# The second layer of six of nine expert blocks in three float32r passes, with the weights split on chip

## The chip, the cores and the metric

One core of one Trainium2 chip runs the whole program in one launch. The metric is the device time of an execution in microseconds (us), the median of several; lower is better. TensorE is called PE below (PEld its weight loads), VectorE DVE, ScalarE ACT, GpSimd POOL, SyncE SP.

## What is computed

Three parts run one after the other on 1536 tokens (two batches of 768): attention with a window and a few sink keys, a mixture of eight experts with one expert per token, and a two-layer network with an exponential unit. In the reference's own names, cut:

```python
# attention, 2 x 8 heads, 768 x 64: keep = sink (pos < 4) or window (0 <= rel < 128)
a = softmax(where(keep, q @ k.T / 8, -1e9));  x = (a @ v) as [1536, 512]
# experts: only tokens with x @ w_skip > 0; one expert each
for e in range(8):                     # w1[e]: 512 x 1024, w2[e]: 1024 x 512
    h = maximum(x[mask] @ w1[e], 0.0)
    y[mask] = gate_w[mask, None] * (h @ w2[e])
x[do_compute] += y
# network: w_in 512 x 2048, w_out 2048 x 512
h = x @ w_in;  g = where(h > 0, h, exp(minimum(h, 0)) - 1);  out = g @ w_out
```

The inputs are float32, but `w_in` and `w_out` arrive as float64, 8 bytes an element.

## The kernel before

**Stages.** Attention goes over 12 tiles of 128 tokens and writes x to a table in DRAM (`xtab`). Then come nine blocks of 128 tokens: one for each of the eight experts, and a ninth (e = 8, `last`) for an expert with more than 128 tokens. Then the network runs in four groups of 512 tokens; each goes through 16 chunks of 128 hidden columns (`layers`: `l1`, the exponential unit `elu`, `l2`).

**One block** (`block`). Its 128 rows are gathered from `xtab` (`gather`, POOL), transposed on PE (`bx`, line 460) and copied to SBUF (`bxe`, line 345). The first layer (`b1`, line 902) is two halves of 16 float32 matmuls with 128 columns; `relu` (lines 910 and 912) takes each half out of PSUM, on ACT or DVE. The second layer (`b2`, line 918) is eight float32 matmuls of 128x512, in two halves of four; the transposes of the next block stand between the halves. `result` (line 933) scales and adds the rows on DVE, `scat` writes them back. The trace shows each float32 matmul as two records, so a half of `b2` is 8 records and a half of `b1` is 32. In block 8 the second layer goes over the two halves of the output columns one after the other (matmuls of 128x256), so that the next stage can begin on the first.

**Weights.** A block has eight tiles of 128x1024 float32 (512 KB): four of w1, four of w2. They live in half places: `places` are 16 buffers of 128x2048, and `halves` their 32 halves. Places 0 to 11 are there from the start; 12 to 15 hold attention's small tiles (`spare`) and are opened when attention ends (`aend`). Six more tiles (`exs`, in `exa` and `exb`) and the four `raw` tiles take some weights too.

**The network's weights.** Each chunk's `w_in` and `w_out` are loaded as float64 into a `raw` tile (`load_f`, lines 736 and 738) and turned into two float32r parts by seven steps (`cv`): ACT reads the high word (line 970), DVE does lines 972, 973, 974 and 976, then a cast to the high part (line 978, ACT or DVE) and the low part as a subtraction (line 290). The products of the network are three float32r matmuls each, `PASSES` = high·high, high·low, low·high (lines 1089 and 1127).

**Start of the network.** Group 0 reads its x from `xtab` (`load_x0`, line 1000, behind the scatter of block 7), transposes it (`x0t`, line 1040), and adds what block 8 changed by two more products (`x0b`, `x0a`, line 1044) of a one-hot matrix with the change in two parts (`dl`, lines 1013 and 1015). Then `split` cuts it into parts (`xe`, lines 1029 and 1031).

**What sets the order.** Every step is named in a plan with its engines, its length, what it follows, its buffers and a due time (`prio`). A list scheduler (`Plan.run`) picks engine, order and buffers from these numbers when the program is built; on the chip each engine goes through its own list in order, and semaphores do the waiting. So a changed length or due time moves other steps as well.

Of the kernel before, what the change touches and what calls it, by code (L numbers as in the profile page):

```python
# [8 lines left out]
F32 = mybir.dt.float32  # L9
# [8 lines left out]
P = 128  # L18
# [40 lines left out]
class Plan:  # L59
# [116 lines left out]
def fused_kernel(  # L176
# [112 lines left out]
    def sub(o, a, b, e):  # L289
# [13 lines left out]
        xg=ring(4, INF), xT=ring(2, INF), hT=ring(2, INF), a=ring(2, INF), r=ring(2), g=ring(3), XT=ring(6), row=ring(6, INF), o2=raws,  # L303
    )
    kinds["R"] = raws
    pl = Plan(kinds)
# [33 lines left out]
    def sl(kind_tiles, key):  # L340
        return kind_tiles[pl.slot[key][1]]
# [421 lines left out]
    opened = halves[2 * NPA:] + exs + [s for n in ("xg", "xT", "hT", "a") for s in kinds[n] if n != "a" or not s[1]]  # L763
# [83 lines left out]
    def first_block():  # L847

        gl = len(GROUPS) - 1
        nl = GROUPS[gl]  # L850
        t0 = NTILE - nl
        add("gid0", {"d": 0.2}, lambda e: nc.vector.tensor_copy(out=gid0, in_=tab[:, 0:1]), [("g", gl - 1, "tab")], 9.3)
        pl.by["g", gl, "mx"]["after"].append("gid0")
        er = lambda: places[NPA + 1][:, 0:DG]

        def early(e):
            nc.gpsimd.indirect_dma_start(
                out=er(), out_offset=None, in_=xtab[0:1 + t0 * P, :],
                in_offset=bass.IndirectOffsetOnAxis(ap=gid0[:, 0:1].bitcast(U32), axis=0),
            )  # L860
        add("early", {"p": 1.1}, early, ["gid0", "zst"] + [("st", x) for x in range(t0)] + [("g", x, "st") for x in range(gl)], 9.4, lat=3.2)

        def gathered(e):
            for i in range(KD):
                nc.tensor.matmul(bk(("bx", 0), 4)[:, i, :], er()[:, i * P:(i + 1) * P], ident, start=(i == 0), stop=False, is_transpose=True)
        add("bx00", {"e": 0.44}, gathered, ["early", ("av", NTILE - 1, 1)], 11.25, need=[("S", ("bx", 0), 1)])
        for i in range(nl):
            t = t0 + i

            def hot(e, i=i):  # L870
                nc.vector.scalar_tensor_tensor(out=hot0[i], in0=iota, scalar=g8["t"][:, i, 0:1], in1=goh[:, i, 0:1].to_broadcast([P, P]), op0=ALU.is_equal, op1=ALU.mult)
            add(("hot0", i), {"d": 0.26}, hot, [("g", gl, "t8")], 11.2)
# [4 lines left out]
            add(("bx", 0) if i == nl - 1 else ("bxo", i), {"e": 0.9}, own, [("bxo", i - 1) if i else "bx00", ("hot0", i), ("fx", t, 0), ("fx", t, 1)], 11.3, use=[("x", t)])  # L877

    def block(e):
        p0 = 20.0 + 10.0 * e  # L880
# [15 lines left out]
        for n in range(2):  # L896
            def layer1(eng, n=n):
                o = bk(("h", e, n), 4)
                for i in range(4):
                    f = 4 * n + i  # L900
                    for kk in range(KD):
                        nc.tensor.matmul(o[:, i, :], w_tile(("w", e, kk))[:, f * P:(f + 1) * P], sl(post["xT"], ("xT", e))[:, kk, :],  # L902
                                         start=(i == 0 and kk == 0), stop=(i == 3 and kk == KD - 1))
            add(("b1", e, n), {"e": 3.55}, layer1, [("bxe", e)] + [("w", e, kk) for kk in range(KD)], p0 + n, need=[("HB", ("h", e, n), 1)],
                use=[("xT", e)] + [("w", e, kk) for kk in range(KD)])

            def relu(eng, n=n):
                o, i = sl(post["hT"], ("hT", e))[:, 4 * n:4 * n + 4, :], bk(("h", e, n), 4)
# [4 lines left out]
            add(("relu", e, n), {"a": 0.6, "d": 0.69}, relu, [("b1", e, n)] + ([("relu", e, 0)] if n else []), p0 + n, need=[] if n else [("hT", ("hT", e), 2)], use=[("h", e, n)])  # L913

            def layer2(eng, fs, c):
                for f in fs:
                    w = w_tile(("w", e, KD + f // 2)).rearrange("p (c n) -> p c n", c=2)[:, f % 2, :]
                    nc.tensor.matmul(bk(("y", e))[:, c], sl(post["hT"], ("hT", e))[:, f, :], w[:, c], start=(f == 0), stop=(f == KF - 1))  # L918
            ws = [("w", e, KD + 2 * n + i) for i in range(2)]
            if not last:  # L920
                add(("b2", e, n), {"e": 3.45}, lambda eng, n=n: layer2(eng, range(4 * n, 4 * n + 4), slice(0, DM)), [("relu", e, n)] + ws + ([("b2", e, 0)] if n else []), p0 + 2 + n,
                    need=[] if n else [("Y", ("y", e), 1)], use=[("hT", e)] + ws)
            else:

# [34 lines left out]
    for c in range(NCH):  # L959
        gate_c = [("b2", c, 1)] if c < NB - 1 else [("b1", NB - 1, 1)]  # L960
        for w in range(2):
            p0 = 24.0 + 10 * c + w if c < 8 else 300 + (c - 8) * 1.0 - 3.0 + 0.5 * w
            f = ("f", c, w)
            add(("lf", c, w), {"s": 0.45}, lambda e, c=c, w=w: load_f(c, w), [chain[-2]], p0 - 12, need=[("R", f, 2)], size=524288)
# [22 lines left out]

    def piece(g, kk):

        i, j = divmod(pl.slot["XT", g, kk][1], 3)  # L990
        if i not in xt_tiles:
            t = post["bp"].tile([P, 3072], F32R, tag=("a", "xh")[i], name=f"xT{i}")
            xt_tiles[i] = t.rearrange("p (j a n) -> p j a n", j=3, a=2)
        return xt_tiles[i][:, j]
# [524 lines left out]
```

## Time and profile before

| | |
|---|---|
| three executions | 536.35, 538.21, 538.85 us; median 538.21 us |
| profiled execution | 538.53 us, of which the profile's span is 536.7 us |
| busy share of the span | PE 96%, PEld 77%, DVE 59%, ACT 33%, POOL 6% |
| mean granted clock of PE | 0.994 |

The span runs from the first to the last instruction. Attention fills it up to about 128 us, the nine blocks to about 262 us, the four groups of the network the rest. A row of the timeline gives start, length, engine, line, operation, operands and how many were merged; the length holds the drain of the last matmul, so the time of a piece is read from its start to the start of the next piece.

### The profile page before, as it was taken

The page shows a single profiled execution, that of the slowest core. Times are in us where ns is not written, and L with a number is a line of the kernel's source. Part 1 is how long each engine was busy: PE and PEld are TensorE (multiplying, and loading weights), DVE is VectorE, ACT ScalarE, POOL GpSimd, SP SyncE. Part 2 cuts the span into 40 slices and gives each one's busy share as a digit, 9 for nine tenths or more (in the row PEclk, how much of TensorE's full clock was granted, in tenths as well). Part 3 has the DMA queues.
Part 4 walks back from the last instruction along what each step waited for, and adds up shares of the span by engine and source line. Part 5 has one row for each costly group of instructions (what it writes and reads, how often), then busy time and mean ns, then how long its engine had stood idle before and what let it go on. Part 6 is the DMA issues. An engine that isn't in the chain of part 4 may idle for free. (4 is left out here: it accounts for less than half of the span.)

```text
span 536.7 us, 8226 instructions
## 1 busy us (share of the span) xinstructions
PE 512.6 (96%) x3087; PEld 411.5 (77%) x3087; DVE 317.5 (59%) x848; ACT 175.6 (33%) x421; POOL 32.2 (6%) x47
## 2 busy tenths in 40 slices
PE   6899999997999999999999999999999999999993
PEld 3678777877777777778788888888888888888882
DVE  6768686876212278886998944454444545445451
ACT  4777677751000123434486520220101112010110
POOL 2000000012110111000000000100000010000000
PEclk9999999998999999999999999999999999999998
DMA  9999999309999967856474000220000002000002
GB/s 171 255 250 309 311 281 336 95 25 342 396 393 395 349 200 237 295 177 197 159 233 157 1 1 0 77 80 1 0 1 0 1 1 79 1 1 0 1 0 85
DMA packets 73155, 79.11 MB, mean 147 GB/s; under 512 B 43089, under 2 KB 51537, under 8 KB 73106
## 3 DMA queue, kind: packets, MB, share of 16 engines
q1 hardware_dynamic: 69826, 73.29, 43.7%
q0 software_dynamic: 1520, 4.99, 2.6%
q8 instruction: 26, 0.43, 0.3%
q10 hardware_dynamic: 1760, 0.22, 0.3%
q14 instruction: 23, 0.19, 0.1%
HBM read 69.82 MB, written 8.66 MB: 146 GB/s over the span
## 5 line engine op out<-in xcount | busy, mean ns | idle before, releaser
L1127 PE MATMUL bank<-m,gt 128*128 128x512 f32 x576 | 139.1, 390 | 0.0
L1089 PE MATMUL bank<-xT,m 128*128 128x512 f32 x576 | 138.3, 389 | 0.0
L1089 PEld LDWEIGHTS bank<-xT,m 128*128 128x128 f32 x576 | 108.1, 188 | 22.5
L1127 PEld LDWEIGHTS bank<-m,gt 128*128 128x128 f32 x576 | 107.8, 188 | 22.2
L1107 ACT ACTIVATE re<-re 128x512 f32<-128x512 f32 x48 | 30.3, 632 | 174.6 <-DVE re L1105 174.4
L1105 DVE TENSOR_SCALAR re<-bank 128x512 f32<-128x512 f32 x38 | 26.3, 692 | 83.7 <-PE bank L1089 83.7
L902 PEld LDWEIGHTS bank<-blk,pl 128*128 128x128 f32 x480 | 55.3, 192 | 3.7 <-issue 2.6
L918 PE MATMUL bank<-pl,blk 128*128 128x512 f32 (+1 forms) x144 | 57.8, 545 | 0.0
L902 PE MATMUL bank<-blk,pl 128*128 128x128 f32 x480 | 56.1, 275 | 0.7 <-ACT blk L345 0.7
L545 ACT ACTIVATE pw<-sm,rm 128x272 f32<-128x272 f32 (+2 forms) x96 | 47.1, 495 | 7.7 <-DVE rm L537 7.7
L1110 DVE SCALAR_TENSOR_TENSOR re<-re,bank 128x512 f32<-128x512 f32 x48 | 32.9, 686 | 26.5 <-ACT re L1107 26.5
L918 PEld LDWEIGHTS bank<-pl,blk 128*128 128x128 f32 x144 | 26.2, 190 | 20.9 <-issue 20.1
L970 ACT ACTIVATE r<-raw 128x512 f32<-128x512 f32 x32 | 21.3, 680 | 61.8 <-DMA raw<-in_moe_w_in_dram 52.3
L537 DVE CUSTOM_DVE_ANT_0 sm<-bank,mk 128x272 f32<-128x272 f32 (+2 forms) x96 | 35.1, 406 | 6.5 <-PE bank L531 3.8
L290 DVE TENSOR_TENSOR gt<-re,gt 128x512 fp32r<-128x512 f32 x44 | 30.4, 692 | 1.3
L531 PE MATMUL bank<-kt,pl 64*128 64x272 f32 (+2 forms) x192 | 26.8, 394 | 1.3 <-DVE rm L537 1.3
L345 ACT COPY PT<-bank 128x512 f32<-128x512 f32 (+1 forms) x40 | 20.6, 550 | 13.4 <-PE bank L559 11.1
L572 PE MATMUL bank<-PT,pl 128*64 128x128 f32 x352 | 24.5, 279 | 0.1
L572 PEld LDWEIGHTS bank<-PT,pl 128*64 128x64 f32 x352 | 18.7, 136 | 5.6 <-issue 3.0
L460 PE MATMUL bank<-ident,pl 128*128 128x128 f32 x96 | 14.8, 279 | 7.8 <-DMA pl<-in_k_dram 5.6
L290 DVE TENSOR_TENSOR m<-r,m 128x512 fp32r<-128x512 f32 x32 | 21.5, 687 | 0.9 <-ACT m L978 0.6
L976 DVE SCALAR_TENSOR_TENSOR r<-raw,r 128x512 int32<-128x512 int32 x32 | 21.8, 687 | 0.3
(186 smaller groups left out, 513.7 us busy)
## 6 DMA issues: line engine op xcount, KB each, us to landing
pl<-in_moe_w_dram SPq DMA_DIRECT2D x62, 512.0 KB
raw<-in_moe_w_in_dram SPq DMA_DIRECT2D x16, 512.0 KB
raw<-in_moe_w_out_dram SPq DMA_DIRECT2D x16, 512.0 KB
pl<-in_k_dram SPq DMA_DIRECT2D x12, 256.0 KB
pl<-in_q_dram SPq DMA_DIRECT2D x12, 256.0 KB
pl<-in_v_dram SPq DMA_DIRECT2D x12, 256.0 KB
xtab<-pl SPq DMA_DIRECT2D x12, 256.0 KB
out_dram<-raw SPq DMA_DIRECT2D x5, 512.0 KB
```

Source lines behind the costliest of these rows:

```text
L290: CE[e].tensor_tensor(out=o, in0=a, in1=b, op=ALU.subtract)
L531: nc.tensor.matmul(o, qT[r, p, :], rhs, start=True, stop=True)
L537: nc.vector.tensor_tensor_reduce(out=sl(sm_t, ("sm", t, h))[:, 0:n], in0=bk(("s", t, h))[:, 0:n], in1=m, scale=-scale, scalar=3.0e38, op0= ...
L545: nc.scalar.activation(out=sl(pw_t, ("pw", t))[:, h, 0:n], in_=sl(sm_t, ("sm", t, h))[:, 0:n], func=ACTF.Exp, bias=rm[:, t, h:h + 1], scal ...
L572: nc.tensor.matmul(o[i * D:(i + 1) * D, p, :], vt[:, h * D:(h + 1) * D], pT[:, (0 if y else c - 2) + i, :], start=(p == 0 and (y == 1 or n ...
L902: nc.tensor.matmul(o[:, i, :], w_tile(("w", e, kk))[:, f * P:(f + 1) * P], sl(post["xT"], ("xT", e))[:, kk, :], start=(i == 0 and kk == 0) ...
L918: nc.tensor.matmul(bk(("y", e))[:, c], sl(post["hT"], ("hT", e))[:, f, :], w[:, c], start=(f == 0), stop=(f == KF - 1))
L1089: nc.tensor.matmul(bk(name), w[:, a, kk, :], x[:, b], start=(kk == 0 and i == 0), stop=(kk == KD - 1 and i == 2))
L1105: nc.vector.tensor_scalar(out=r, in0=pt, scalar1=-1.0, scalar2=0.0, op0=ALU.mult, op1=ALU.max)
L1107: nc.scalar.activation(out=r, in_=r, func=ACTF.Exp, scale=-1.0)
L1110: nc.vector.scalar_tensor_tensor(out=r, in0=r, scalar=-1.0, in1=pt, op0=ALU.add, op1=ALU.max)
L1127: nc.tensor.matmul(bk(("acc", g, i)), gt[:, a, i * P:(i + 1) * P], w[:, b, :], start=(c == 0 and j == 0), stop=(c == NCH - 1 and j == 2))
```

## The change

For six blocks, e in `RB` = 1, 2, 3, 4, 5 and 8, the second layer becomes three float32r passes. Each w2 tile is cut on the chip into a high part (`hi`, a cast, ACT or DVE) and a low part (`lo`, a subtraction on DVE), kept as one tile `hl` of 128x2x1024 float32r in places 12 to 15: four `hl` tiles, as many as one block has, opened when block 0's `bx` is done and no longer used for weights until block 8 ends. `relu` gives the high part of h on ACT, a new step `rell` on DVE the low part. Blocks 0, 6 and 7 stay in float32. A w2 tile is free again when its low part is made, no longer when the matmuls have read it. The due times of the conversions (`cv`) go from 24 + 10c for the first eight chunks to 297 + c for all, those of their loads to 12 + 10c; the tiles of the expert stage are laid out anew (`xa`, `xb`, `hs`). The core of the diff:

```diff
+    RB = (1, 2, 3, 4, 5, 8)
-    opened = halves[2 * NPA:] + exs + [s for n in ("xg", "xT", "hT", "a") ...]
+    opened = exs + [s for n in ("xg", "xT", "hT", "a") ...]
...
+    def hl(key):
+        i = pl.slot[key][1]
+        if i not in hl_tiles:
+            hl_tiles[i] = place_p.tile([P, 2048], F32R, tag=f"pl{i}", name=f"hl{i}").rearrange("p (a n) -> p a n", a=2)
+        return hl_tiles[i]
...
+            if fine:
+                def relu_low(eng, n=n):
+                    h = sl(post["hT"], ("hT", e, n))
+                    nc.vector.scalar_tensor_tensor(out=h[:, 1], in0=bk(("h", e, n), 4), scalar=0.0, in1=h[:, 0].bitcast(F32), op0=ALU.max, op1=ALU.subtract)
+                add(("rell", e, n), {"d": 0.7}, relu_low, [("relu", e, n)], p0 + n, use=[("h", e, n)])
+                for i in (2 * n, 2 * n + 1):
...
+                    add(("hi", e, i), {"a": 1.02, "d": 0.66}, lambda eng, key=key, wt=wt: CPY[eng](out=hl(key)[:, 0], in_=wt()), [("w", e, KD + i)], p0 - 5 + i, port=True, need=[("HL", key, 2 if last else 1)])
+                    add(("lo", e, i), {"d": 1.16}, lambda eng, key=key, wt=wt: sub(hl(key)[:, 1], wt(), hl(key)[:, 0].bitcast(F32), eng), [("hi", e, i)], p0 - 5 + i, port=True, use=[("w", e, KD + i)])
...
+                    if fine:
+                        w = hl(("hl", e, f // 2)).rearrange("p a (c n) -> p a c n", c=2)[:, :, f % 2, c]
+                        h = sl(post["hT"], ("hT", e, f // 4))
+                        for j, (a, b) in enumerate(PASSES):
+                            nc.tensor.matmul(y, h[:, a, f % 4, :], w[:, b], start=(f == 0 and j == 0), stop=(f == KF - 1 and j == 2))
...
-            p0 = 24.0 + 10 * c + w if c < 8 else 300 + (c - 8) * 1.0 - 3.0 + 0.5 * w
+            pf, p0 = (12.0 + 10 * c + w if c < 8 else 280 + c + 0.5 * w), 297 + c + 0.5 * w
```

**Where the order moves.** DVE between the first halves of the second layers of blocks 1 and 2, before: `blk` is the relu output or the transposed x, `r` the rows of a block.

```order
L912 TENSOR_SCALAR blk<-bank_90 128x512
L912 TENSOR_SCALAR blk<-bank_91 128x512
L345 COPY blk<-bank_96 128x512
L933 SCALAR_TENSOR_TENSOR r_1489<-bank_94,r_1489 128x512
L912 TENSOR_SCALAR blk<-bank_92 128x512
L912 TENSOR_SCALAR blk<-bank_89 128x512
```

The same place now; `hr` is h in parts, `hl` the split w2 tile, line 292 the subtraction, 938 the cast, 933 `rell`, 968 `result`.

```order
L933 SCALAR_TENSOR_TENSOR hr<-bank_90,hr 128x512
L933 SCALAR_TENSOR_TENSOR hr<-bank_91,hr 128x512
L938 CAST hl_1547<-pl_73 128x1024
L347 COPY blk<-bank_96 128x512
L292 TENSOR_TENSOR hl_1547<-pl_73,hl_1547 128x1024
L292 TENSOR_TENSOR hl_1550<-pl_73,hl_1550 128x1024
L968 SCALAR_TENSOR_TENSOR r_1491<-bank_94,r_1491 128x512
L292 TENSOR_TENSOR hl_1571<-pl_74,hl_1571 128x1024
L292 TENSOR_TENSOR hl_1578<-pl_74,hl_1578 128x1024
L933 SCALAR_TENSOR_TENSOR hr<-bank_92,hr 128x512
L933 SCALAR_TENSOR_TENSOR hr<-bank_89,hr 128x512
```

One cast and four subtractions of 128x1024 stand between the two blocks, around `result`; the other three casts are on ACT.

PE at the end of block 8, before: lines 1040 and 1044 are `x0t` and `x0b`/`x0a`, line 918 the second layer's second output half, 1089 the network.

```order
L1040 MATMUL bank_89<-ident,exb 128x128 x4
L1044 MATMUL bank_90<-oh,delta 128x512
L1044 MATMUL bank_91<-oh,delta 128x512
L918 MATMUL bank_93<-pl_64,blk 128x256 x4
L1044 MATMUL bank_90<-oh,delta 128x512
L1044 MATMUL bank_91<-oh,delta 128x512
L918 MATMUL bank_93<-pl_65,blk 128x256 x4
L1044 MATMUL bank_92<-oh,delta 128x512
L1044 MATMUL bank_89<-oh,delta 128x512
L1089 MATMUL bank_95<-xT_2269,m_1872 128x512 x6
L1044 MATMUL bank_92<-oh,delta 128x512
L1044 MATMUL bank_89<-oh,delta 128x512
```

The same place now; line 948 is the split second layer, 1076 `x0t`, 1080 `x0b` and `x0a`.

```order
L948 MATMUL bank_93<-hl_1571,hr 128x256 x6
L948 MATMUL bank_93<-hl_1578,hr 128x256 x6
L1076 MATMUL bank_90<-ident,exb 128x128 x4
L1076 MATMUL bank_91<-ident,exb 128x128 x4
L1076 MATMUL bank_92<-ident,exb 128x128 x4
L1076 MATMUL bank_89<-ident,exb 128x128 x4
L1080 MATMUL bank_90<-oh,delta 128x512
L1080 MATMUL bank_91<-oh,delta 128x512
L1080 MATMUL bank_92<-oh,delta 128x512
L1080 MATMUL bank_89<-oh,delta 128x512
L1080 MATMUL bank_90<-oh,delta 128x512
L1080 MATMUL bank_91<-oh,delta 128x512
```

The whole second layer of block 8 now stands ahead of the transposes of x; two more products of `x0a` and then the network follow.

## Rows read from the trace of the kernel before

**Rows 1.** Three stretches: length, busy us (records) by engine, clock, DMA share, GB/s.
```profile
128.61:244.33 115.72, 115.72 (x672) 84.72 (x673) 60.92 (x125) 23.20 (x38) 17.05 (x16) 1.00 0.86 308
244.33:264.39 20.06, 19.50 (x127) 17.39 (x126) 17.86 (x34) 8.35 (x15) 1.82 (x2) 1.00 0.58 197
264.39:350.00 85.61, 85.61 (x387) 71.04 (x386) 59.86 (x108) 36.22 (x61) 3.15 (x3) 1.00 0.24 77
```
**Rows 2.** Timeline of PE, second layer of block 1.
```profile
150.31 3.60 PE L918 MATMUL bank<-pl,blk 128*128 128x512 f32 x8
153.74 0.60 PE L460 MATMUL bank<-ident,r 128*128 128x128 f32 x4
154.18 3.60 PE L918 MATMUL bank<-pl,blk 128*128 128x512 f32 x8
```
**Rows 3.** Timeline of PE, the network in group 0.
```profile
290.28 2.88 PE L1089 MATMUL bank<-xT,m 128*128 128x512 f32 x12
293.00 2.88 PE L1127 MATMUL bank<-m,gt 128*128 128x512 f32 x12
```
**Rows 4.** Timeline of PE, block 8 and the start of group 0.
```profile
244.33 7.31 PE L902 MATMUL bank<-blk,pl 128*128 128x128 f32 x64
251.47 3.62 PE L918 MATMUL bank<-pl,blk 128*128 128x256 f32 x16
255.08 1.97 PE L1040 MATMUL bank<-ident,exb 128*128 128x128 f32 x16
256.80 0.71 PE L1044 MATMUL bank<-oh,delta 128*128 128x512 f32 x2
259.54 1.89 PE L918 MATMUL bank<-pl,blk 128*128 128x256 f32 x8
261.99 0.73 PE L1044 MATMUL bank<-oh,delta 128*128 128x512 f32 x2 [0.56 <-ACT delta L1013]
262.56 1.54 PE L1089 MATMUL bank<-xT,m 128*128 128x512 f32 x6
264.39 1.78 PE L1089 MATMUL bank<-xT,m 128*128 128x512 f32 x7
```
**Rows 5.** Groups by form: busy us, mean ns, idle us before, releaser.
```profile
L345 ACT COPY PT<-bank 128x512 f32<-128x512 f32 x33 | 18.1, 588 | 7.4 <-PE bank L559 6.4 <-ACT PT L345 0.5 <-ACT pw L545 0.3
L345 ACT COPY PT<-bank 128x256 f32<-128x256 f32 x7 | 2.5, 371 | 6.0 <-PE bank L559 4.7 <-issue 1.3
L1112 DVE CAST gt<-re 128x512 fp32r<-128x512 f32 x34 | 14.5, 427 | 1.2
L290 DVE TENSOR_TENSOR m<-r,m 128x512 fp32r<-128x512 f32 x32 | 21.5, 687 | 0.9 <-ACT m L978 0.6
L611 DVE TENSOR_TENSOR pl<-bank,den 128x256 f32<-128x256 f32 x24 | 10.1, 422 | 2.5 <-PE bank L603 2.0
L933 DVE SCALAR_TENSOR_TENSOR r<-bank,r 128x512 f32<-128x512 f32 x9 | 6.7, 749 | 11.1 <-PE bank L918 11.1
L910 ACT ACTIVATE blk<-bank 128x512 f32<-128x512 f32 x8 | 4.8, 597 | 20.7 <-PE bank L902 16.7 <-issue 3.9
L345 DVE COPY blk<-bank 128x512 f32<-128x512 f32 x4 | 2.8, 692 | 11.9 <-PE bank L460 11.9
```
**Rows 6.** Line 974 alone: one record for each half chunk converted.
```profile
180.00:262.00 82.00, 13.52 (x20) 1.00 0.71 234
262.00:312.00 50.00, 8.25 (x12) 1.00 0.35 111
```
**Rows 7.** Issues of SP, from start us and length.
```profile
136.63 1.76 SPq L718 DMA_DIRECT2D pl<-in_moe_w_dram  x4
249.26 0.37 SPq L1000 DMA_DIRECT2D exb<-xtab  x1
```
**Rows 8.** Who waited for loads in the stretch 128 to 311: total us, times, longest.
```profile
ACT r L970 <- DMA raw<-in_moe_w_out_dram: 1.1, 2, 0.7
PEld bank L1040 <- DMA exb<-xtab: 0.4, 1, 0.4
```

More of the change, by code (lines that the diff above doesn't have):

```diff
@@ L302, in fused_kernel @@
         nat=ring(4), v=ring(4), qT=ring(2), sm=ring(4), pw=ring(2), PT=ring(4), psT=ring(1), psc=ring(1), oT=ring(2), x=ring(2),
-        xg=ring(4, INF), xT=ring(2, INF), hT=ring(2, INF), a=ring(2, INF), r=ring(2), g=ring(3), XT=ring(6), row=ring(6, INF), o2=raws,
+        xg=ring(4, INF), xT=ring(2, INF), hT=ring(2, INF), a=ring(2, INF), r=ring(2), g=ring(3), XT=ring(6), row=ring(6, INF), o2=raws, HL=[[INF, i] for i in range(NPA, NPL)],
     )
@@ L905, in block @@
                 use=[("xT", e)] + [("w", e, kk) for kk in range(KD)])
+            fine = e in RB
             def relu(eng, n=n):
-                o, i = sl(post["hT"], ("hT", e))[:, 4 * n:4 * n + 4, :], bk(("h", e, n), 4)
+                o, i = sl(post["hT"], ("hT", e, n))[:, 0] if fine else post["h0"][n], bk(("h", e, n), 4)
                 if eng == "a":
@@ L912, in relu @@
                     nc.vector.tensor_scalar(out=o, in0=i, scalar1=0.0, scalar2=None, op0=ALU.max)
-            add(("relu", e, n), {"a": 0.6, "d": 0.69}, relu, [("b1", e, n)] + ([("relu", e, 0)] if n else []), p0 + n, need=[] if n else [("hT", ("hT", e), 2)], use=[("h", e, n)])
+            add(("relu", e, n), {"a": 0.6} if fine else {"a": 0.6, "d": 0.69}, relu, [("b1", e, n)] + ([("relu", e, 0)] if n else []), p0 + n,
+                need=[("hT", ("hT", e, n), 2 if last else 1)] if fine else [], use=[("h", e, n)] if not fine else [])
@@ L915, in layer2 @@
             def layer2(eng, fs, c):
                 for f in fs:
-                    w = w_tile(("w", e, KD + f // 2)).rearrange("p (c n) -> p c n", c=2)[:, f % 2, :]
-                    nc.tensor.matmul(bk(("y", e))[:, c], sl(post["hT"], ("hT", e))[:, f, :], w[:, c], start=(f == 0), stop=(f == KF - 1))
-            ws = [("w", e, KD + 2 * n + i) for i in range(2)]
+                    y = bk(("y", e))[:, c]
+                    if fine:
[3 more added lines that the diff above has]
+                            nc.tensor.matmul(y, h[:, a, f % 4, :], w[:, b], start=(f == 0 and j == 0), stop=(f == KF - 1 and j == 2))
+                    else:
+                        w = w_tile(("w", e, KD + f // 2)).rearrange("p (c n) -> p c n", c=2)
+                        nc.tensor.matmul(y, post["h0"][f // 4][:, f % 4, :], w[:, f % 2, c], start=(f == 0), stop=(f == KF - 1))
@@ L920, in block @@
+            ws = [("lo", e, 2 * n + i) if fine else ("w", e, KD + 2 * n + i) for i in range(2)]
+            wu = [("hl", e, 2 * n + i) if fine else ("w", e, KD + 2 * n + i) for i in range(2)]
+            src = [("rell" if fine else "relu", e, n)] + ws
             if not last:
-                add(("b2", e, n), {"e": 3.45}, lambda eng, n=n: layer2(eng, range(4 * n, 4 * n + 4), slice(0, DM)), [("relu", e, n)] + ws + ([("b2", e, 0)] if n else []), p0 + 2 + n,
-                    need=[] if n else [("Y", ("y", e), 1)], use=[("hT", e)] + ws)
-            else:
-                add(("b2", e, 0) if n else ("b2x", e), {"e": 1.75}, lambda eng, n=n: layer2(eng, range(4 * n, 4 * n + 4), slice(0, DM // 2)), [("relu", e, n)] + ws + ([("b2x", e)] if n else []), p0 + 2 + n,
-                    need=[] if n else [("Y", ("y", e), 5)])
+                add(("b2", e, n), {"e": 2.75 if fine else 3.45}, lambda eng, n=n: layer2(eng, range(4 * n, 4 * n + 4), slice(0, DM)), src + ([("b2", e, 0)] if n else []), p0 + 2 + n,
+                    need=[] if n else [("Y", ("y", e), 1)], use=([("hT", e, n)] if fine else []) + wu)
+            else:
+                add(("b2", e, 0) if n else ("b2x", e), {"e": 1.47}, lambda eng, n=n: layer2(eng, range(4 * n, 4 * n + 4), slice(0, DM // 2)), src + ([("b2x", e)] if n else []), p0 + 2 + n,
+                    need=[] if n else [("Y", ("y", e), 5)], use=[("hT", e, n)] + wu)
@@ L927, in block @@
                 if n:
                     for h in range(2):
-                        add(("b2", e, 1) if h else ("b2y", e), {"e": 1.75}, lambda eng, h=h: layer2(eng, range(4 * h, 4 * h + 4), slice(DM // 2, DM)), [("b2y", e) if h else ("b2", e, 0)], p0 + 4 + h,
-                            use=[("hT", e)] + [("w", e, KD + 2 * h + i) for i in range(2)])
+                        add(("b2", e, 1) if h else ("b2y", e), {"e": 1.47}, lambda eng, h=h: layer2(eng, range(4 * h, 4 * h + 4), slice(DM // 2, DM)), [("b2y", e) if h else ("b2", e, 0)], p0 + 4 + h,
+                            use=[("hT", e, h)] + [("hl", e, 2 * h + i) for i in range(2)], opens=halves[2 * NPA:] if h else ())
@@ L961, in fused_kernel @@
         for w in range(2):
[L962 removed]
+            pf, p0 = (12.0 + 10 * c + w if c < 8 else 280 + c + 0.5 * w), 297 + c + 0.5 * w
             f = ("f", c, w)
[L964 removed]
+            add(("lf", c, w), {"s": 0.45}, lambda e, c=c, w=w: load_f(c, w), [chain[-2]], pf, need=[("R", f, 2)], size=524288)
             chain.append(("lf", c, w))
@@ L988, in piece @@
     def piece(g, kk):
[L990 to L994, printed above, removed]
+        j = pl.slot["XT", g, kk][1]
+        tag, n, j = ("a", 3, j) if j < 3 else ("xb", 2, j - 3) if j < 5 else ("xa", 1, 0)
+        if tag not in xt_tiles:
+            t = post["bp"].tile([P, n * 1024], F32R, tag=tag, name="xT" + tag)
+            xt_tiles[tag] = t.rearrange("p (j a n) -> p j a n", j=n, a=2)
+        return xt_tiles[tag][:, j]
     def x0_tile():
```

14 lines of the change are left out of this document (10 added, 4 removed).

## The prediction

> **What bounds the kernel now.** I read the busy times by stretch first. From the first layer of block 0 to block 8 PE is busy 115.72 of 115.72 us, and in the network's next 85.61 us the same; only the 20.06 us in which block 8 hands over to the network hold 0.56 us of idle PE [rows 1]. The reader is to see that the second half of the program is one unbroken queue on PE, at a granted clock of 1.00, with DVE at 53% and 70% beside it. So PE work that is taken away there is time, as long as nobody else becomes late. The timeline of PE gives what a piece costs, as the distance between starts; the groups by form give what DVE and ACT pay; the waits say who was ever late for PE.
>
> **What goes away on PE.** Half a second layer in float32 (four matmuls of 128x512, 8 records) runs from 150.31 to 153.74, 3.43 us [rows 2]: 0.86 us a matmul. The same product in three float32r passes is what the network does: 12 passes from 290.28 to 293.00, 2.72 us, 0.227 us each [rows 3]. A half so loses 3.43 - 2.72 = 0.71 us. Blocks 1 to 5 have ten halves: 7.1 us.
>
> Block 8 has four pieces of four matmuls of 128x256. Two took from 251.47 to 255.08, 3.61 us with 0.4 of wait for a load at the end [rows 4, 8], so 1.6 each; the last one ran from 259.54 to 261.99 less 0.56 idle, 1.9 with its drain. 8 records of 128x512 take 3.43, and half the columns make 1.72, which lies between and which I take. No row shows a float32r pass of 256 columns. Its lower bound is half of 0.227, 0.113 us; the upper bound, if the narrow pass gains nothing, is 0.227. Float32 goes down by half with the columns, so I take the lower end with a little on top, 0.12: 12 x 0.12 = 1.44 a piece, and 4 x (1.72 - 1.44) = 1.1 us less. At the upper bound the four pieces grow by 4 x (2.72 - 1.72) = 4.0 us.
>
> The Trainium skill, on its page "TensorE: Matmul & The Clock Gate", section "Back-to-back issue gap", gives a warm matmul N/2.4 + 2.5 ns, 216 ns at 512 columns and 109 at 256. By that the sum would be 10 x (3.43 - 12 x 0.216) + 4 x (1.72 - 12 x 0.109) = 8.4 + 1.6 = 10.0 us. The row of just this form has 0.227, 5% more, and I keep to it.
>
> **What is added, and what hides it.** Per split block: four `hi` casts and four `lo` subtractions of 128x1024, two `rell`; the relus only change engine or output. ACT copies 256 columns in 0.371 and 512 in 0.588 [rows 5]; with the same slope a `hi` on ACT is 0.588 + 2 x 0.217 = 1.02. A cast of 512 on DVE is 0.427, so a `hi` there lies between that and 0.85; I take 0.70. A two-source step is 0.422 at 256 and 0.687 at 512, so a `lo` is between 0.69 and 1.37, by the slope 0.687 + 2 x 0.265 = 1.22, which I take. `rell` reads PSUM like `result`, 0.749. Together DVE gets 0.70 + 4 x 1.22 + 2 x 0.75 = 7.1 us a block and loses up to two relus.
>
> What matters is the chain between two blocks, since the four `hl` tiles are all in use. Let T be the end of the first half of `b2` in block e. The transposes take 0.44 [rows 2], the second half 2.72, the next first layer 251.47 - 244.33 = 7.14 [rows 4]: the next `b2` can start at T + 10.3. DVE from T + 0.2 (I allow 0.2 us for each hand-over): `hi` to 0.9, the copy of x (0.692) to 1.6, two `lo` to 4.0, `result` (0.749) to 4.8, two `lo` to 7.2. Their casts on ACT start at T + 3.4 and are done at 5.4. The first half of the next first layer ends at T + 6.7; relu on ACT (0.597) to 7.5, `rell` to 8.3. PE wants it at T + 10.3: 2.0 us to spare. The second `rell` waits for the end of the first layer, 10.3 + 0.2 + 0.6 + 0.75 = 11.9, and is wanted at 10.3 + 2.72 + 0.44 = 13.5. With the upper bounds of `hi` and `lo` the first `rell` still ends by about T + 8.8. So I cost the split at nothing. If that cover were gone, each block would wait by the excess, five times. Queued behind these DVE steps are conversions only, and the `result` whose scatter nobody reads soon.
>
> Weights: the loads that went to places 12 to 15 at the end of attention now wait for the first `lo`s, a few us, and the tiles in question are those of block 4, far away. From there a tile of 0.524 MB is issued at about the pace at which places become free; the stretch moved 308 GB/s [rows 1], and eight tiles in a block of 14.4 - 1.4 = 13.0 us are 323 GB/s. I cost that at nothing as well. The w2 tiles come free earlier than before.
>
> Conversions: before, 20 of the 32 half chunks had passed line 974 at 262 us and 12 came later [rows 6]. DVE is taken by splits in blocks 4, 5 and 8, 7.1 us each, some 21 us; a half chunk costs DVE two one-source steps (0.43) and three two-source steps (0.69), 2.9 us with the cast on ACT, so about 7 half chunks slip, and 18 to 19 of them lie in group 0. There PE needs 16 x 5.44 = 87 us (two pieces of 2.72 a chunk). DVE needs 19 x 2.9 = 55 us and two steps of 0.69 a chunk for the unit, 22: 77 in all. It fits, with 10 us to spare, and PE has six chunks or so in hand at the start, 33 us of work. Cost: nothing, but the cover is thin.
>
> **The end of block 8.** Before, from 244.33 to 264.39 [rows 4]: 20.06 us. Now: 7.14 + 4 x 1.44 + `x0t` (256.80 - 255.08 = 1.72) + eight products of 0.23 (from 12 passes in 2.72) = 16.5, and six passes of 0.227, 1.4: 17.8 of work. Since all of `b2` stands ahead, nothing covers the chain behind the last `x0a`: with E the end of `b2`, `x0a` is done with its second strip at E + 3.1; then DVE casts it (to 4.0) and makes two low parts (0.69 each, to 5.3), while PE is through with `x0a` at E + 3.6. So the first network passes wait about 1.1 us, which the wait for `delta` (0.56) and the rest of the idle time had cost before. The load of x is no longer the last thing: it was issued at 249.26 and awaited at 255.08, 10.75 us after the block's start [rows 4, 7], and is now wanted 7.14 + 5.8 = 12.9 after it, though it stands behind one more load that waits for a `rell`. Net of this stretch: 17.8 + 1.1 = 18.9 against 20.06, 1.2 us less, the 1.1 from above within it.
>
> **Sum.** 7.1 + 1.2 = 8.3 us off the profiled execution of 538.5: 530.2. That execution lies 0.3 above the median of the runs shown (538.21), so I forecast 530 us for the median.
>
> **Rivals.**
> 1. Part is given back. The load of x comes late or the thin covers tear in one or two places (the hand-over, the first elus behind conversions): 1.5 to 5 us of wait, about 533. For it: DVE is the busiest helper, 17.86 of 20.06 us in the hand-over [rows 1]. Against: PE lost under 1 us there before. Passes of 256 columns that gain nothing belong here too: 530 + 1.1 + 4.0 = 535.
> 2. The narrower gap of the page: 528.2 by 10.0 us. Against it stands the row of the same form.
> 3. No gain: the chain of the split is 3.7 us longer than worked out, 2.0 to use up the slack and 1.65 more in each of five blocks, 8.3 in all; 538. For it: the one set of `hl` tiles. Against: even the upper bounds leave over 1 us.
> 4. Slower: DVE becomes the bound of group 0. Its in-order queue holds the units behind conversions, and those behind their float64 loads. If each of nine remaining chunks held DVE 3.5 us for its load, 32 us, 10 of which are spare, PE would wait 22 us, and the end comes at 552. It decides at 10 / 9 = 1.1 us a chunk for any loss, at 2.0 for a loss of the whole gain (18.3 / 9), at 2.3 for slower by 2.7. For it: 77 of 87 us, and more where relu and cast of the unit fall on DVE. Against: before, ACT waited for such a load 0.7 us at most once they ran [rows 8], and PE was never idle in that stretch at 70% of DVE.
>
> **How the numbers follow.** 0.5% is 2.7 us, about what a measurement here can tell from no change. Forecast 0.63; rival 1 0.19; rival 2 0.05; rival 3 0.07; rival 4 0.06. Faster by over 0.5%: the forecast, rival 2 and nearly all of rival 1, 0.87. Within 0.5%: rival 3, 0.07. Slower: rival 4, 0.06. The low end is rival 2, 528.2; the upper end, 534.4, takes in most of rival 1. Above it lie rivals 3 and 4 and the rest of 1, in all 0.17.
>
> **What the profile would show.** Right: halves of `b2` of 2.7 us in blocks 1 to 5, PE without idle time up to block 8; one wait of about 1 us ahead of the first network passes, put down to DVE; `lo` near 1.2 us; more of line 974 after the start of group 0. Wrong: PE waiting for `hl` or `hr` at a block's second layer (rival 3), PE idle ahead of line 1163 in group 0 (rival 4), or a pace of passes other than 0.227 (rival 2), above all at 256 columns.

## The result and the profile after

The changed kernel took 530.65 us (median of 4 runs, 528.48 to 532.63), the kernel before 538.45 beside it: a ratio of 0.986 (95% interval 0.9829 to 0.9891), 7.8 us less. Forecast were 530 us. The profiled execution took 530.91 us with a span of 529.1; before it was 538.53 with 536.7. The two spans differ by 7.6 us, and starts on PE say where. Both marks of a stretch are the same piece of work in both kernels; the network's seventh pass is the first one behind the six that the kernel before runs ahead of its last `x0a` products [rows 4].

| stretch, by starts on PE | before, us | after, us | gain |
|---|---|---|---|
| start to block 1's first layer | 143.16 | 143.45 | -0.29 |
| blocks 1 to 5 | 143.16 to 215.43 | 143.45 to 208.95 | 6.77 |
| blocks 6 and 7, float32 in both | 215.43 to 244.33 | 208.95 to 237.86 | -0.01 |
| block 8 to the network's seventh pass | 244.33 to 264.39 | 237.86 to 258.22 | -0.30 |
| from there to the last 36 passes | 264.39 to 519.62 | 258.22 to 513.44 | 0.01 |
| the last 36 passes and the end | 519.62 to 536.7 | 513.44 to 529.1 | 1.4 |

So the five blocks hold the gain on PE, and block 8 gained nothing: it takes 0.30 us longer than before. The end is the same work in both, and its last store is issued 9.27 us after its start in both:

```profile
258.22 1.55 PE L1125 MATMUL bank<-xTa,m 128*128 128x512 f32 x6
513.44 8.32 PE L1163 MATMUL bank<-m,gt 128*128 128x512 f32 x36
522.71 0.34 SPq L1184 DMA_DIRECT2D out_dram<-raw  x1
```

And the kernel before:

```profile
519.62 8.32 PE L1127 MATMUL bank<-m,gt 128*128 128x512 f32 x36
528.89 0.45 SPq L1148 DMA_DIRECT2D out_dram<-raw  x1
```

What differs is the time behind that store, 7.8 us before and 6.4 after. From the start of the last 36 passes to the end the traces of the changed kernel and its variants below range from 15.7 to 17.1 us, whatever the edit; there is one trace of the kernel before, so whether its longer end belongs to it stays open. Over several executions the picture is the same: in ten of twelve comparisons, this one and those below, the ratio shows more gain than the traces' stretch from block 1 to the last 36 passes (6.47 us here), by 2.3 us on the mean. So some 2 us of what was measured seem to lie ahead of block 1 or behind the last passes, and no run says in what.

The stretches beside [rows 1], in the same columns. The second holds one network pass, where the kernel before has six in its own, so that their lengths, 19.09 and 20.06, can't be compared:

```profile
126.83:237.86 111.03, 109.18 (x713) 91.96 (x714) 76.37 (x127) 40.58 (x56) 17.97 (x16) 1.00 0.84 295
237.86:256.95 19.09, 17.40 (x139) 16.21 (x137) 16.54 (x33) 9.21 (x16) 2.46 (x2) 1.00 0.67 227
256.95:342.56 85.61, 85.61 (x386) 71.02 (x387) 73.27 (x135) 46.02 (x76) 2.59 (x2) 1.00 0.36 114
```

DVE, the third pair of numbers, now works 73.27 of 85.61 us in the network's first stretch, where it had 59.86, and PE is still never idle there. What is new is 1.85 us of idle PE in the first row. The timeline of PE, blocks 0 to 2 (start us, length, and in brackets the idle time before and who ended it):

```profile
126.83 7.41 PE L915 MATMUL bank<-blk,pl 128*128 128x128 f32 x64 [0.67 <-ACT blk L347]
...
139.52 0.66 PE L462 MATMUL bank<-ident,r 128*128 128x128 f32 x4 [1.85 <-DMA r<-xtab,gidx]
...
143.45 7.31 PE L915 MATMUL bank<-blk,pl 128*128 128x128 f32 x64
150.51 3.01 PE L948 MATMUL bank<-hl,hr 128*128 128x512 f32 x12
153.36 0.60 PE L462 MATMUL bank<-ident,r 128*128 128x128 f32 x4
153.72 3.02 PE L948 MATMUL bank<-hl,hr 128*128 128x512 f32 x12
156.57 7.30 PE L915 MATMUL bank<-blk,pl 128*128 128x128 f32 x64
163.63 2.98 PE L948 MATMUL bank<-hl,hr 128*128 128x512 f32 x12
```

Against [rows 2] a half is 12 passes from 150.51 to 153.36, 2.85 us, and a block repeats after 13.12 us here and 13.10 on the mean of five, where it was 14.45. Block 8, against [rows 4]:

```profile
237.86 7.31 PE L915 MATMUL bank<-blk,pl 128*128 128x128 f32 x64
244.92 4.56 PE L948 MATMUL bank<-hl,hr 128*128 128x256 f32 x36
250.56 1.69 PE L948 MATMUL bank<-hl,hr 128*128 128x256 f32 x12 [1.08 <-DVE delta L1051]
252.09 1.91 PE L1076 MATMUL bank<-ident,exb 128*128 128x128 f32 x16
253.76 2.11 PE L1080 MATMUL bank<-oh,delta 128*128 128x512 f32 x8
255.84 0.49 PE L1125 MATMUL bank<-xTa,m 128*128 128x512 f32 x1
256.95 2.36 PE L1125 MATMUL bank<-xTa,m 128*128 128x512 f32 x9 [0.61 <-DVE xTa L1067]
```

The groups by form of the new steps, from 126.83 to 256.95, against [rows 5] (busy us, mean ns of one, idle time before):

```profile
L292 DVE TENSOR_TENSOR hl<-pl,hl 128x1024 fp32r<-128x1024 f32 x20 | 23.9, 1219 | 3.2 <-ACT hl L938 3.2
L933 DVE SCALAR_TENSOR_TENSOR hr<-bank,hr 128x512 fp32r<-128x512 f32 x12 | 8.3, 692 | 17.1 <-ACT hr L925 17.1
L938 DVE CAST hl<-pl 128x1024 fp32r<-128x1024 f32 x4 | 2.8, 691 | 1.0 <-DMA pl<-in_moe_w_dram 0.9
```

And the casts on ACT in the same columns, which wait for the `hl` tile to come free or for the weights:

```profile
L938 ACT CAST hl<-pl 128x1024 fp32r<-128x1024 f32 x15 | 15.4, 1046 | 14.5 <-PE bank L948 8.7 <-DMA pl<-in_moe_w_dram 5.8
```

And the conversions, line 1009 alone, against [rows 6]:

```profile
180.00:256.00 76.00, 9.44 (x14) 1.00 0.76 253
256.00:306.00 50.00, 8.33 (x13) 1.00 0.47 148
```

14 half chunks instead of 20 are done when the network begins; the last one passes that line at 324.75.

### The profile page after: what moved, and what is told of

Read it like the earlier page. It is cut to its first block, busy times and chain, and to the rows that moved or that the text cites. A ratio compares the mean times of both kernels' runs of the same rounds, so it can differ in the third digit from the quotient of the medians.

```text
span 529.1 us, 8427 instructions
## 1 busy us (share of the span) xinstructions
PE 506.6 (96%) x3143; PEld 418.8 (79%) x3143; DVE 345.3 (65%) x874; ACT 203.6 (38%) x455; POOL 33.4 (6%) x47
## 4 chain that ended last, share of the span: by engine, by line
PE 88%; DMA 7%; DVE 2%; issue 1%; ACT 1%; POOL 0%; DVEq 0%; ACTq 0%
PE bank L1125 25%; PE bank L1163 25%; PE bank L915 11%; PE bank L948 6%; DMA pl<-in_k_dram 4%; PE bank L574 4%; PE bank L533 4%; PE bank L951 3%; PE bank L462 3%; PE bank L605 2%; PE bank L561 2%; PE bank L579 1%; PE bank L560 1%; DMA r<-xtab,gidx 1%; DMA pl<-xtab,gid 1%
## 5 line engine op out<-in xcount | busy, mean ns | idle before, releaser
L1125 PE MATMUL bank<-xTa,m 128*128 128x512 f32 x384 | 97.9, 390 | 0.6 <-DVE xTa L1067 0.6
L1125 PEld LDWEIGHTS bank<-xTa,m 128*128 128x128 f32 x384 | 72.0, 188 | 16.3 <-DVE xTa L1067 0.9
L1141 DVE TENSOR_SCALAR re<-bank 128x512 f32<-128x512 f32 x35 | 24.2, 692 | 74.9 <-PE bank L1125 74.9
L1125 PE MATMUL bank<-xTxb,m 128*128 128x512 f32 x144 | 40.4, 389 | 0.0
L948 PE MATMUL bank<-hl,hr 128*128 128x512 f32 (+1 forms) x168 | 36.3, 367 | 1.1 <-DVE delta L1051 1.1
L948 PEld LDWEIGHTS bank<-hl,hr 128*128 128x128 f32 x168 | 27.7, 189 | 5.5 <-DVE delta L1051 1.3
L1125 PEld LDWEIGHTS bank<-xTxb,m 128*128 128x128 f32 x144 | 27.0, 188 | 5.6
L292 DVE TENSOR_TENSOR hl<-pl,hl 128x1024 fp32r<-128x1024 f32 x20 | 23.9, 1219 | 3.2 <-ACT hl L938 3.2
L347 ACT COPY PT<-bank 128x512 f32<-128x512 f32 (+1 forms) x40 | 20.6, 550 | 13.3 <-PE bank L561 11.0
```

What stands on the lines that cost most here:

```text
L292: CE[e].tensor_tensor(out=o, in0=a, in1=b, op=ALU.subtract)
L948: nc.tensor.matmul(y, h[:, a, f % 4, :], w[:, b], start=(f == 0 and j == 0), stop=(f == KF - 1 and j == 2))
L1125: nc.tensor.matmul(bk(name), w[:, a, kk, :], x[:, b], start=(kk == 0 and i == 0), stop=(kk == KD - 1 and i == 2))
L1141: nc.vector.tensor_scalar(out=r, in0=pt, scalar1=-1.0, scalar2=0.0, op0=ALU.mult, op1=ALU.max)
```

## The experiments

Each is one edit on the changed kernel. The kernel before took 537.6 to 540.5 us beside the different sets, so times are compared by the ratio to the kernel before, and stages by the traces. A block 8 of 19.1 us (17.9, 20.0, 20.6) is taken to the start of the unbroken passes, which in these traces have one pass ahead of them; where the mark lies elsewhere, the time to the seventh pass is given, 20.36 us in the changed kernel.

**The parts in block 8 alone.**
```
-    RB = (1, 2, 3, 4, 5, 8)
+    RB = (8,)
```


> Only block 8 keeps its second layer in float32r parts, blocks 1 to 5 are float32 again; memory layout, loads and the new due times of the conversions stay. Theory (PE is the queue, each of the five blocks gave 1.36 us, read from the block period 14.46 -> 13.10 us): 530.65 + 6.8 = 537.4 us, ratio to before about 0.998; the rest of the change is worth about 1 us. Rival A (the five blocks gave what the issue gap of the page says, 1.68 us each): 539.0 us. Rival B (the moved conversions or the new layout are the larger part of the gain, the parts little): clearly below 536.

Measured: ratio 0.9964 (0.9937 to 0.9991). By the ratios the edit takes away 1.0% of the time, 5.6 us with over 2 us of uncertainty. The trace is sharper: the block period is 14.45 us again in all five blocks, 6.77 us. Rival A's 539.0 would be 1.001 and lies outside. Rival B can't be excluded by the interval's lower end alone; the trace shows no stage on PE between block 1 and the last 36 passes that gained without the parts. Block 8 to the seventh pass took 21.83 us here, 1.8 more than before: PE waited 2.09 us for the load of x, since the planner set its transposes ahead of the last quarter. So the 5.6 us hold some 1.5 us of block 8, and the ratio alone doesn't price the five blocks. And a kernel that is 2.0 us faster by its ratio, with a stretch on PE that is 1.8 us longer, has some 3.7 us from elsewhere, with an uncertainty of about 1.5; what the rest of the change is worth there stays open.

**A fourth pass.**
```
-                        for j, (a, b) in enumerate(PASSES):
+                        for j, (a, b) in enumerate(PASSES + ((1, 1),)):
```


> A fourth float32r pass (low part times low part) for each product of the split second layers: 40 passes of 512 columns in blocks 1 to 5, 16 of 256 in block 8, nothing else. Theory (PE has no idle time there, so every pass is paid in full): 40 x 0.227 to 0.2375 + 16 x 0.12 to 0.127 = 11.0 to 11.5 us more, 541.7 to 542.2; a block's period 13.10 + 1.81 to 1.90 us. Rival (the split on DVE and ACT, or the weights' loads, set the block's period already): less than half of that, under 536.

Measured: ratio 1.002 (0.9993 to 1.0047), 542.55 us. The timeline of PE, block 1:

```profile
151.89 3.91 PE L948 MATMUL bank<-hl,hr 128*128 128x512 f32 x16
155.64 0.60 PE L462 MATMUL bank<-ident,r 128*128 128x128 f32 x4
155.99 3.92 PE L948 MATMUL bank<-hl,hr 128*128 128x512 f32 x16
159.75 0.49 PE L915 MATMUL bank<-blk,pl 128*128 128x128 f32 x3
```

A half of 16 passes takes 3.75 us, one of 12 takes 2.85: 0.225 a pass. The block period goes from 13.10 to 14.91, 0.227 for each of 8 passes, and block 8 grows by 1.8 us for 16. So every pass is paid in full: PE is the bound, and the rival falls. By the traces' stages that makes 10.8 us, just below the 11.0 expected; the ratios give some 9 with over 2 us of uncertainty.

**Blocks 6 and 7 as well.**
```
-    RB = (1, 2, 3, 4, 5, 8)
+    RB = (1, 2, 3, 4, 5, 6, 7, 8)
```


> Blocks 6 and 7 are split as well. Theory (1.36 us a block as long as the covers hold): 530.65 - 2.7 = 527.9 us, ratio to before 0.980. Rival (DVE is short in group 0: 14 us of further splits push some 5 more half chunks of conversions behind the start of group 0, 24 x 2.9 + 22 = 92 us of DVE work against 87 of PE): 531 to 536 us, with idle PE ahead of the network's second layer in group 0.

Measured: ratio 0.9833 (0.9795 to 0.9871). Both theories hold, each in its place. The block period is 13.09 us in blocks 6 and 7 also, 2.7 us less in sum. Block 8 to the seventh pass takes 18.71 us, 1.65 less than in the changed kernel: here the transposes stand ahead of the last quarter and the load of x is there. But from the seventh pass to the last 36 it takes 260.0 us, where it was 255.2, and there PE now waits:

```profile
PE bank L1163 <- ACT gt L1148: 1.1, 2, 0.6
PE bank L1125 <- ACT m L1013: 0.8, 2, 0.4
PE bank L1163 <- DVE gt L292: 0.3, 2, 0.2
```

The waits lie at 308 to 330 us, at the end of the conversions. They are 2.2 of the 4.8 us; the rest is passes that stand further apart around them. Rival 4 of the prediction is no fancy: it begins two blocks further on, with 4.8 of its 22 us.

**The slack of the split.** One low part of the four, or all four, are computed twice.
```
-  sub(hl(key)[:, 1], wt(), hl(key)[:, 0].bitcast(F32), eng)
+  [sub(hl(key)[:, 1], wt(), hl(key)[:, 0].bitcast(F32), eng) for _ in range(2 if key[2] == 0 else 1)]
```
For all four the count is `range(2)`.


> One of the four low parts of each split block is computed twice, into the same place: 1.13 to 1.22 us more on DVE a block. Theory (the chain of the split has 2.0 us to spare: rell done at 161.66, wanted at 163.63): no wait of PE, block period 13.10, time within 1 us of the control. Rival (the chain is tight, what is added to it is paid): 5 x 1.2 = 6 us slower.

> All four low parts of each split block are computed twice: 4.5 to 4.9 us more on DVE a block. Theory (2.0 us to spare, the rest is paid by PE waiting for rell or hl ahead of the second layer): 2.5 to 3.4 us in each of blocks 2 to 5, 0 to 2 in block 8, in all 10 to 16 us: 541 to 547; block period 15.6 to 16.5. Rival (DVE is at 65% of the span, so that there is room for it on average): 531.

Measured: with one, ratio 0.9865 (0.9817 to 0.9913), no wait for `hl` or `hr`, periods of 13.1 us in blocks 1 to 5. Blocks 6 and 7 take 0.97 us more together, with a wait of 0.69 ahead of block 7: its copy of x stands on ACT behind a cast for block 8, which here waited 6.19 us for its weights. With all four, 546.57 us in one run, 16.5 more than the control, of which blocks 2 to 7 are 13.7 and a later start of block 1 and a longer end the rest. The waits:

```profile
PE bank L948 <- DVE hr L933: 6.8, 4, 2.5
PE bank L915 <- ACT blk L347: 2.9, 2, 2.2
```

So an engine at 69% of the span can be the bound. Blocks 2 and 3 grew by 1.5 us only, less than expected. In the changed kernel DVE is idle ahead of `rell`, which the theory left out:

```profile
160.97 0.69 DVE L933 SCALAR_TENSOR_TENSOR hr<-bank,hr 128x512 fp32r<-128x512 f32 x1 [1.08 <-ACT hr L925]
```

Four more `lo` are 4.9 us; 1.1 of them fall into this idle time, 2.0 into the room that was worked out, and two of the 12 passes (0.45) don't read the low part of `h` and run ahead of the wait. That leaves 1.4 us. Blocks 4 and 5 grew by 2.2 and 4.3, with conversions among the splits, and with a granted clock of 0.61 from 211.96 to 216.30 in block 5 (last section); 6 and 7, with a copy of x for block 7 that came 2.2 us late, by 4.1 together.

**The changed kernel again.**

> The changed kernel once more, as it is, beside the others on their chip. Theory: ratio to before 0.986 again, and the stages that hold its gain repeat in a second profile: block period 13.10 us in blocks 1 to 5, 19.1 us for block 8. What need not repeat is the 1.85 us wait for block 1's gather: if it hangs on when block 0 starts, a start 1.8 us later shows none, with the same start of block 1's first layer (about 17 us behind the end of the gate).

Measured: 530.04 us, ratio 0.985 (0.9805 to 0.9896). Block period 13.10, block 8 19.08. The wait for block 1's gather is 0.81 us this time, with block 0 starting at 126.81, no later than in the first trace. So the expected case of a later start did not come up; block 1 began at 142.39, 1.06 us earlier, since its gather landed 1.05 us earlier, at 138.42 instead of 139.47.

**Block 8's deltas later.**
```
-  add(("dl", 0, h), {"a": 0.37}, lambda e, h=h: delta(e, 0, h), [("b2", L8, h)], PB + 3.5, use=[("y", L8)])
+  add(("dl", 0, h), {"a": 0.37}, lambda e, h=h: delta(e, 0, h), [("b2", L8, 1)], PB + 3.5, use=[("y", L8)])
```


> Both halves of block 8's delta wait for the whole second layer instead of their half of it, so that no delta stands between the third and the last quarter. Theory (the 1.08 us wait ahead of the last quarter is the chain ACT delta, DVE delta on the first half of the same bank, put in order between two writes of that bank; behind the quarter it is hidden by the 1.7 us of transposes of x): the wait goes, 0.5 to 1.1 us less, block 8 takes 18.0 to 18.6 us instead of 19.1. Rival (the chain only moves: the first product with delta or the low parts of the network's input wait as much): 19.1 us again, no change in time.

Measured: the wait is gone, block 8 takes 17.88 us, 1.2 less, as the theory has it:

```profile
239.63 7.31 PE L915 MATMUL bank<-blk,pl 128*128 128x128 f32 x64
246.69 6.00 PE L948 MATMUL bank<-hl,hr 128*128 128x256 f32 x48
252.53 1.91 PE L1076 MATMUL bank<-ident,exb 128*128 128x128 f32 x16
254.19 2.11 PE L1080 MATMUL bank<-oh,delta 128*128 128x512 f32 x8
256.28 0.51 PE L1125 MATMUL bank<-xTa,m 128*128 128x512 f32 x1
257.51 3.50 PE L1125 MATMUL bank<-xTa,m 128*128 128x512 f32 x14 [0.72 <-DVE xTa L1067]
```

48 narrow passes in 5.84 us are 0.122 each. The time doesn't show the gain: ratio 0.9875 (0.9827 to 0.9924), the control's interval holds it. In this execution block 1 began 2.2 us later than in the control, at a granted clock of 0.50 from the gate to 132 us, and blocks 6 and 7 took 0.7 us longer, with a wait of 0.45 for block 7's copy of x.

**The store ahead of the gathers.** First, the weight loads wait for it:
```
+        if 2 * NPA <= i < 2 * NPA + 6:
+            after.append(("g", len(GROUPS) - 1, "st"))
```


> The six weight loads that are issued just ahead of the last 1 KB store of gate weights into the token table now wait for that store's issue; nothing else. Theory (that store, 7.7 us from issue to landing behind 1.5 MB of weights, holds back the gathers, and block 1's gather is what PE waits 1.85 us for ahead of its transposes): the wait goes, 530.65 - 1.8 = 528.8 us. Rival A (the gather waits for something else, or its own 6 us of landing set the time): 530.6. Rival B (the later loads are missed by block 3 or 4): above 531.5.

Measured: ratio 0.9826 (0.9788 to 0.9864). The store landed 3.5 us after its issue instead of 7.7, the wait for the gather went, although block 0 began at 127.06, and block 1's first layer began at 141.62. But the moved loads also changed the planner's order in block 8: its transposes stood ahead of the last quarter and waited 2.52 us for the load of x, and to the seventh pass the block took 23.36 us, 3.0 more. What one wait gave, the other took, and more; the ratio is too coarse to show either.

Then the store on ACT's queue, with the later deltas:
```
-  G("st", {"s": 0.45}, lambda e: nc.sync.dma_start(
+  G("st", {"s": 0.45}, lambda e: (nc.scalar if final else nc.sync).dma_start(
```


> Two edits on the changed kernel: block 8's deltas wait for the whole second layer (as before in the experiment on them), and the last 1 KB store of gate weights into the token table is issued by ACT's queue instead of SP's, where 1.5 MB of weights stand ahead of it. Theory (both waits are what the profile calls them): no wait ahead of the last quarter, block 8 at 17.9 us; the store lands early, the gathers start as soon as their indices are there, about 128 us, and PE's wait of 0.8 to 1.85 us for block 1's gather goes: 527.5 to 529 us, ratio 0.981 to 0.983. Rival (the store lands as late on the other queue, since the 16 engines are shared): the gather's wait stays, ratio 0.984.

Measured: ratio 0.9822 (0.9797 to 0.9847), and neither wait is left: the transposes of block 1 begin at 139.22 right behind the first half of block 0, and block 8 takes 17.88 us. For the gather that shows little: block 0 began at 128.54, at a granted clock of 0.50, and in the control the gather of block 1 had landed at 138.42, so that these transposes need not have waited for it either. Here it landed at 136.92. The evidence on the store is the run before this one. The store was issued 0.35 us ahead of the gate's last ranks on PE (120.7 against 121.05), where it stood 0.43 behind them (122.93 against 122.50), and landed in 6.6 us instead of 7.7. By the middle of its interval this is 0.3 to 0.4% below the changed kernel, but the intervals overlap. With block 6 split as well:

> The same with block 6 split too. Theory: another 1.36 us less in block 6; 3 more half chunks of conversions slip, 22 of them behind the start of group 0: 22 x 2.9 + 22 = 86 us of DVE against 87 of PE, at the edge: 526 to 528 us. Rival (with blocks 6 and 7 the network lost 2.2 us to idle PE at 308 to 330 us; one block does too): no better than without block 6.

Measured: 0.9816 (0.9792 to 0.9839), no better. Block 6 took 13.1 us, but the load of x came 1.52 us late for transposes that the planner had set ahead of the last quarter again, and block 8 took 20.6.

**The old due times of the conversions.**
```
-  pf, p0 = (12.0 + 10 * c + w if c < 8 else 280 + c + 0.5 * w), 297 + c + 0.5 * w
+  p0 = 24.0 + 10 * c + w if c < 8 else 300 + (c - 8) * 1.0 - 3.0 + 0.5 * w
+  pf = p0 - 12
```


> The changed kernel with the old due times of the float64 conversions, so that they come ahead of the splits where both are ready. Theory (the due times are worth nothing by themselves, the chain of the split keeps its 2.0 us): within 1.5 us of the control, ratio 0.984 to 0.988, more half chunks done before group 0. Rival (2.9 us of conversion in front of a low part or a rell uses up the 2.0 us): PE waits for hr or hl in blocks 3 to 5, 3 to 8 us slower, ratio 0.991 or above.

Measured: ratio 0.9914 (0.9882 to 0.9947), so the theory is wrong and the rival right in size: about 3 us of the gain go by the ratios, and 3.8 us of PE time from block 1 to the last 36 passes by the traces. Its waits:

```profile
PE bank L1077 <- DMA exb<-xtab: 2.6, 1, 2.6
...
PE bank L948 <- DVE hr L933: 0.7, 1, 0.7
```

Only 0.7 us of it is the chain of the split that the rival named. The most lies in block 8, 23.3 us long to the seventh pass, 2.9 more. The last run put its transposes back:

```
-  ["lx0", ("b1", L8, 1)], PB + 2.5 + 0.01 * kk
+  ["lx0", ("b2", L8, 1)], PB + 2.5 + 0.01 * kk
```


> The old due times again, but the transposes of x wait for the whole second layer of block 8, as they stand in the changed kernel. With the old due times alone block 8 took 21.9 us, 2.8 more than in the changed kernel: its transposes stood ahead of the last quarter and waited 2.63 us for the load of x, and TensorE ran at half its clock after that wait. Theory (the loss of the old due times is for the most part that place in PE's row, and 0.7 us the conversions ahead of rell): block 8 at 19 to 20.5 us, the time 1.5 to 3 us below that of the old due times, ratio 0.986 to 0.989. Rival (the loss is DVE's work in the wrong order, wherever PE waits for it): ratio 0.991 again.

Measured: block 8 took 20.0 us, as expected, and the stretch from block 1 to the last 36 passes 2.0 us less than with the old due times alone. But the ratio stayed at 0.9926 (0.9901 to 0.9951), as the rival has it. In its trace block 1 began 3.3 us later than in the control, at a granted clock of 0.57 in the first 4.9 us of block 0, and the end behind the start of the last 36 passes was 1.0 us longer. Whether these have to do with the edit stays open, and with it how much of the loss is the order in block 8.

## Why the prediction came out right

The number was right, 530 against 530.65, and so was the larger of its two terms. The smaller one, block 8, did not come, and time outside the stretch on PE stands in for it, in the profiled pair an end that is 1.4 us shorter, for which no step has a term. That the sum still fits is luck.

- **The ten halves, 7.1 us: 6.77.** The price of a pass was right; the fourth pass cost 0.225 to 0.227, and 0.227 was read from [rows 3]. But a half took 2.85 us in block 1, 0.13 more than 12 passes of the network. The first layer and the transposes, 7.06 and 0.36 us there, give back 0.08 each. So a block, which would have taken 7.14 + 0.44 + 2 x 2.72 = 13.02 us [rows 2, 4], took 13.10 on the mean. Since a fourth pass costs 0.225 us, the surplus of a half stands at its two ends, where PE changes between float32 and float32r; no run separates it further.
- **The narrow pass, 0.12 us: 0.122.** The lower end of the bounds was right.
- **The page's gap, rival 2.** By the formula on the page "TensorE: Matmul & The Clock Gate" of the Trainium skill, section "Back-to-back issue gap", which gives it there for an isolated matmul, a pass would have cost 0.216 us and a block saved 1.68, both estimates; the traces have 0.225 to 0.227 and 1.35. The measurement decides against it.
- **The split, costed at nothing.** `hi` 0.69 on DVE and 1.046 on ACT (0.70 and 1.02 were estimated), `lo` 1.219 (1.22), `rell` 0.692 (0.75). In block 2 `rell` was done at 161.66 and PE wanted it at 163.63: 1.97 us to spare, 2.0 were worked out. Adding one `lo` a block cost blocks 1 to 5 nothing, adding four cost blocks 2 to 7 13.7 us. Rival 3 falls.
- **Conversions, costed at nothing.** 7 of 20 half chunks were to slip: 6 did; 18 or 19 were to lie in group 0: 18 did. DVE worked 73.27 of 85.61 us there, PE was not idle. That the cover is thin showed with two more blocks. But the step took the slip as DVE's load alone and gave the due times no price; by the ratios they are worth some 3 us. In the traces 2.9 of 3.8 us lie in block 8, whose order on PE hangs on them; putting the transposes back returned 2.0 us in the trace, but not in the ratio.
- **Block 8, 1.2 us less: 0.30 more.** The 18.9 us of the prediction hold six network passes, as the 20.06 before do, so they answer to 20.36 and not to 19.09. The wait ahead of the network was put at 1.1 us and cost about 1.0: the first six passes and the wait among them took from 255.84 to 258.22, 2.38 us, where six passes alone are 1.36. What the step left out is a stop of 1.08 us between the third and the last quarter: the four quarters took 7.17 us, 5.76 were put. A `delta` of the first half reads the bank into which these quarters write other columns, and it stands between them in program order; with the deltas behind the last quarter the stop went, the quarters took 5.84 us, and block 8 to the seventh pass 19.15, 0.9 below the kernel before. So the price of a narrow pass was right and the order was not followed through.
- **What no step foresaw: the gather of block 1.** Before, block 0 began at 128.61 and the gather was no wait; after, it began at 126.83 and PE waited 1.85 us for it. That earlier start is not the change's: it goes with a granted clock of 1.00 there instead of 0.61. The chain of the 1 KB store, 7.7 us from issue to landing, and the gathers behind it sets when block 1 can begin, whatever PE gains ahead of it; with the store ahead of the weights the wait went. To the start of block 1 the two traces differ by 0.29 us.

## What to carry to other kernels

Where PE is an unbroken queue, an edit of its passes is worth the difference of two start-to-start distances from the trace, and in blocks 1 to 5 that held within 5%. A stretch is compared only between marks with the same work behind them: five network passes on the wrong side of a mark made 0.30 us of loss in block 8 look like 0.97 of gain. Further, the room of the steps that feed PE is read from their chain, not from their engine's share. Before a second such edit is made, count what the helper has left in the stretch into which it pushes work. And where a planner sets the order, look at the stretch with the most dependencies after any edit: here block 8 changed by up to 3 us with edits that lay elsewhere.

## What was not expected of the hardware

After some long waits PE came back at half its clock, 0.50 in the clock column or 1.2 of 2.4 GHz, and the price of the wait grew. With all low parts doubled, ten passes behind a wait of 2.47 us took 4.14 us, and behind one of 1.91 us 2.58:

```profile
196.11 2.58 PE L948 MATMUL bank<-hl,hr 128*128 128x512 f32 x10 [1.91 <-DVE hr L933]
...
211.96 4.14 PE L948 MATMUL bank<-hl,hr 128*128 128x512 f32 x10 [2.47 <-DVE hr L933]
```

With the old due times the 16 transposes of x behind 2.63 us of wait took 3.32 us instead of 1.91, in a stretch whose granted clock was 0.50:

```profile
254.00:255.45 1.45, 1.45 (x9) 1.45 (x8) 0.00 (x0) 0.00 (x0) 0.00 (x0) 0.50 0.98 334
```

A wait of 2.09 us in block 8 of the first experiment was not followed by it. The same clock also came ahead of block 0, where PE waits 2.04 us for the gate, in some executions and not in others: 0.61 at 124 to 128 us before, 1.00 after and in the control, 0.50 with the later deltas. The matmuls between the gate and block 0 took from 123.68 to 127.69 us before, 4.01 us, and from 123.52 to 125.91 after, 2.39. That moves the start of block 0 by 1.6 us between two traces, and with it what a gain ahead of the gathers is worth.
